# Decode attention over two key/value caches: the order of every engine fixed by hand, and all loads on one queue

## The chip, the cores and the metric

The kernel runs on one core of a Trainium2 chip. The metric is device microseconds of one execution. Most executions of a kernel agree within 0.3%. A profile is one such execution; its span is 1.5 to 2 us shorter than the time of that execution.

Engines: PE multiplies matrices, DVE does elementwise work and reductions, ACT does exponentials and copies, SP issues loads. Sixteen DMA engines move the data. "The end of the stream" is the end of the last K or V packet in the trace's list of DMA packets, and "the tail" is the rest of the span after it.

## The reference, cut to what matters

Two independent decode problems, A and B, with one query each; the outputs stand side by side.

```python
q = (x @ wq).reshape(32 heads, 128)
scores = einsum("hd,hkd->hk", q, k) * 128 ** -0.5     # A: 16384 keys, B: the last 4096
p = softmax(scores)
o = einsum("hk,hkd->hd", p, v)
out = o.reshape(1, 4096) @ wo                          # 512 columns
```

K and V of one A head are 4 MB each; four B heads together are as large. The whole input is 352 MB, read once.

## The kernel before

A chunk is 64 keys on each of 128 partitions, half an A head or two B heads. DVE multiplies K by q and adds the halves, PE sums what is left with an identity matrix (`red`), DVE reduces, ACT takes the exponential, and PE does p.v. with 64 matmuls. A scheduler orders the instructions. K, wq and wo are loaded from SP, V and x from ACT.

```python
def _scores(nc, cx, kv, q_of, pieces):
    ...
        nc.vector.tensor_tensor(out=prod[...], in0=kv[...], in1=q..., op=ALU.mult)      # L73
    nc.vector.tensor_tensor(out=half, in0=prod[..., 0:64], in1=prod[..., 64:128], op=ALU.add)  # L80
    ... 8 matmuls with ident into red                                                   # L90
    nc.vector.tensor_reduce(out=sc, in_=red, ...)                                       # L98
    ... exp on ACT into p_sb, row sums into cs

def _pv(nc, cx, acc, p_sb, vt, cs, first, last):
    o_ps, s_ps = acc
    for c in range(n):
        nc.tensor.matmul(o_ps[0:1, :], lhsT=p_sb[:, c:c+1], rhs=vt[:, c, :], ...)       # L117
    nc.tensor.matmul(s_ps[0:1, 0:1], lhsT=cs, rhs=cx.ones_col[:, 0:1], ...)             # L124

# main loop: head by head; after every fourth A head a group of four B heads
    for h in range(stA.H):
        ...
        _head_A(nc, cx, stA, h)              # K on nc.sync, V on nc.scalar
        if h % (2 * G) == 0:
            _load_wo(nc, cx, stA, h)
        if h % G == G - 1:
            if (h // G) % 2 == 0:
                _load_wo(nc, cx, stB, h - G + 1)
            _group_B(nc, cx, stB, h - G + 1)
```

There are two buffers each for K, V and wo, and one for `s_ps`. `...` on a line of its own, or in an index, marks a cut.

The softmax here doesn't subtract the row's maximum and nothing guards it: scores larger than these inputs give would overflow.

## Time and profile before

858.1 us is the median of four runs (857.0 to 859.0).

| | before |
|---|---|
| span | 855.4 us |
| mean load rate | 413 GB/s |
| DVE busy, PE busy | 69%, 66% |
| end of the stream | 841.1 us |
| tail | 14.3 us |

The page's DMA rows give the busy share in tenths and the rate in 40 slices, and then each queue with its packets, MB and share of the 16 engines:

```profile
DMA  9999999999999899999999999999999999999992
GB/s 392 423 424 379 420 432 432 426 426 427 434 422 435 334 431 439 424 429 419 433 421 437 423 425 431 427 429 409 419 429 427 434 421 428 432 427 430 401 398 87
...
q1 hardware_dynamic: 11684, 184.56, 50.7%
q10 hardware_dynamic: 9504, 167.78, 46.3%
```

The load engines are busy nearly all the time, at about 427 GB/s in most slices. Only the dips and the last slice leave anything to win. Here are the windows of three dips (busy time of each engine, then PE's clock, the DMA share and GB/s):

```profile
60.00:70.00 10.00, 7.73 (x74) 6.59 (x75) 8.48 (x7) 0.78 (x4) 0.00 (x0) 0.70 0.74 282
280.00:290.00 10.00, 4.63 (x34) 2.94 (x34) 9.97 (x6) 0.35 (x2) 0.00 (x0) 0.50 0.68 292
290.00:300.00 10.00, 9.94 (x157) 8.96 (x154) 6.53 (x2) 0.36 (x1) 0.00 (x0) 0.94 0.91 362
```

The end of the chain of waits (start, duration, what) shows the last B heads, one per 2.35 us, and then the output product:

```profile
846.03 0.37 ACT orow L139
846.44 0.29 PE oc_ps L144 x4
846.73 1.32 PE o_ps L117 x22
848.04 0.06 PE s_ps L124 x2
848.19 0.17 DVE recip L137
848.38 0.37 ACT orow L139
...
851.69 1.04 PE outB L156 x4
```

### The profile page before, as it was taken

To read this page: it belongs to the slowest core of one execution; us is meant where nothing else is said; L and a number is where in the kernel's file an instruction comes from. 1 tells how busy PE (TensorE), PEld (TensorE's weight loads), DVE (VectorE), ACT (ScalarE), POOL (GpSimd) and SP (SyncE) were. 2 spreads that over 40 slices of the span, in tenths; PEclk is the share of its full clock that TensorE was granted. 3 is DMA by queue.
4 is the path that set the end of the run, shared out by engine and by line. 5 is a ranking of instruction groups with operands and counts; after the bars stand their busy time and mean duration, and the time that the engine had idled before them with its cause. 6 is when DMAs were issued, how large, how long until landed. Compare 5 with 4: busy or idle time off the path is not lost.

```text
span 855.4 us, 13729 instructions
## 1 busy us (share of the span) xinstructions
PE 565.1 (66%) x6335; PEld 425.1 (50%) x6336; DVE 590.3 (69%) x346; ACT 64.7 (8%) x275; POOL 0.7 (0%) x6
## 2 busy tenths in 40 slices
PE   3146657768782677758755586758877657673877
PEld 1034535565640566446644464536755536453656
DVE  0469775975783866947967397656969378785791
ACT  2000020100010000100000000000001000010001
POOL 0000000000000000000000000000000000000000
PEclk9577888889896699969978897788998779886999
DMA  9999999999999899999999999999999999999992
GB/s 392 423 424 379 420 432 432 426 426 427 434 422 435 334 431 439 424 429 419 433 421 437 423 425 431 427 429 409 419 429 427 434 421 428 432 427 430 401 398 87
DMA packets 21245, 353.20 MB, mean 413 GB/s; under 512 B 2498, under 2 KB 2500, under 8 KB 4548
## 3 DMA queue, kind: packets, MB, share of 16 engines
q1 hardware_dynamic: 11684, 184.56, 50.7%
q10 hardware_dynamic: 9504, 167.78, 46.3%
q8 instruction: 49, 0.80, 0.4%
q14 instruction: 8, 0.07, 0.0%
HBM read 352.32 MB, written 0.00 MB: 412 GB/s over the span
## 4 chain that ended last, share of the span: by engine, by line
DMA 55%; DVE 21%; PE 15%; issue 7%; another core or an unknown queue 1%; ACT 1%; ACTq 0%; SPq 0%; DVEq 0%
DMA kt<-in_A_k_cache_dram 26%; DMA vt<-in_A_v_cache_dram 16%; DVE prod L73 12%; PE o_ps L117 10%; DVE half L80 6%; DMA kt<-in_B_k_cache_dram 6%; DMA xTB<-in_B_x_dram 4%; PE red L90 3%; DMA vt<-in_B_v_cache_dram 3%; DVE sc L98 3%; ACT orow L139 0%; PE oc_ps L144 0%; DVE recip L137 0%; PE outB L156 0%
## 5 line engine op out<-in xcount | busy, mean ns | idle before, releaser
L117 PE MATMUL o_ps<-vt,p_sb 128*1 128x128 bf16 x5120 | 351.9, 236 | 112.2 <-DMA vt<-in_A_v_cache_dram 82.6
L117 PEld LDWEIGHTS <-p_sb 128*1 128x1 bf16 x5120 | 333.9, 92 | 132.8 <-issue 112.1
L73 DVE TENSOR_TENSOR prod<-kt,qallA 128x8192 bf16<-128x8192 bf16 x64 | 282.9, 4420 | 90.4 <-DMA kt<-in_A_k_cache_dram 89.5
L90 PE MATMUL red<-half,ident 128*128 128x512 bf16 x640 | 169.0, 403 | 84.5 <-DVE half L80 84.4
L80 DVE TENSOR_TENSOR half<-prod 128x4096 bf16<-128x4096 bf16 x80 | 182.6, 2283 | 0.6
L90 PEld LDWEIGHTS <-ident 128*128 128x128 bf16 x640 | 58.8, 101 | 124.5 <-issue 69.7
L73 DVE TENSOR_TENSOR prod<-kt,qallB 128x4096 bf16<-128x4096 bf16 x32 | 72.0, 2284 | 11.1 <-DMA kt<-in_B_k_cache_dram 9.4
L98 DVE TENSOR_REDUCE sc<-red 128x64 f32<-128x512 f32 x80 | 54.1, 680 | 37.0 <-PE red L90 35.6
L144 PEld LDWEIGHTS <-orow 1*32 1x32 bf16 x256 | 12.2, 111 | 103.6 <-ACT orow L139 60.1
L139 ACT ACTIVATE orow<-o_ps,recip 1x128 bf16<-1x128 f32 x64 | 22.8, 356 | 514.5 <-DVE recip L137 467.7
L144 PE MATMUL oc_ps<-one,orow 1*32 1x1 bf16 x256 | 17.4, 171 | 54.1 <-ACT orow L139 53.7
L137 DVE RECIPROCAL recip<-s_ps 1x1 f32<-1x1 f32 x64 | 9.6, 150 | 50.1 <-PE s_ps L124 50.1
L102 ACT ACTIVATE p_sb<-sc 128x64 bf16<-128x64 f32 (+1 forms) x96 | 23.4, 244 | 251.8 <-DVE sc L98 251.5
L124 PE MATMUL s_ps<-ones_col,cs 128*1 128x1 f32 x192 | 18.3, 165 | 18.2 <-DVE recip L137 17.6
L153 DVE CAST oc<-oc_ps 128x4 bf16<-128x4 f32 x16 | 2.5, 155 | 39.0 <-PE oc_ps L144 39.0
L124 PEld LDWEIGHTS s_ps<-ones_col,cs 128*1 128x1 f32 x192 | 11.4, 84 | 31.5 <-DVE recip L137 19.7
L45 PE MATMUL q_ps<-wq_t,xbA 128*128 128x512 bf16 x32 | 9.4, 466 | 13.5 <-DVE xbA L40 13.5
L102 ACT ACTIVATION_READ_ACCUMULATOR p_sb<-sc 128x1 f32 x96 | 17.9, 186 | 0.1
L156 PE MATMUL outA<-wo_t,oc 128*1 128x512 bf16 x32 | 12.3, 528 | 4.9 <-DVE oc L153 4.9
L40 DVE COPY xbB<-xTB 128x128 bf16<-128x128 bf16 x4 | 0.6, 222 | 20.1 <-DMA xTB<-in_B_x_dram 20.1
L45 PEld LDWEIGHTS <-xbA 128*128 128x128 bf16 x32 | 3.7, 116 | 18.6 <-DVE xbA L40 13.6
L156 PEld LDWEIGHTS <-oc 128*1 128x1 bf16 x64 | 5.7, 99 | 12.9 <-DVE oc L153 5.8
(17 smaller groups left out, 32.3 us busy)
## 6 DMA issues: line engine op xcount, KB each, us to landing
vt<-in_A_v_cache_dram ACTq DMA_DIRECT2D x32, 4096.0 KB, 22.1
kt<-in_A_k_cache_dram SPq DMA_DIRECT2D x32, 4096.0 KB, 24.2
kt<-in_B_k_cache_dram SPq DMA_DIRECT2D x32, 1024.0 KB, 20.0
vt<-in_B_v_cache_dram ACTq DMA_DIRECT2D x32, 1024.0 KB, 25.0
wq_t<-in_A_wq_dram SPq DMA_DIRECT2D x1, 4096.0 KB, 12.2
wo_t<-in_A_wo_dram SPq DMA_DIRECT2D x4, 1024.0 KB, 21.2
wo_t<-in_B_wo_dram SPq DMA_DIRECT2D x4, 1024.0 KB, 27.5
wq_t<-in_B_wq_dram SPq DMA_DIRECT2D x1, 4096.0 KB, 16.1
```

What stands on the lines that cost most here:

```text
L45: nc.tensor.matmul(q_ps[:, :], lhsT=xb[:, c, :], rhs=wq_t[:, c, j * 512 : (j + 1) * 512], start=(c == 0), stop=(c == KC - 1),)
L73: nc.vector.tensor_tensor(out=prod[:, k0 : k0 + n, :], in0=kv[:, k0 : k0 + n, :], in1=q.rearrange("p (o d) -> p o d", o=1).broadcast_to([P ...
L80: nc.vector.tensor_tensor(out=half[:, :, :], in0=prod[:, :, 0 : DH // 2], in1=prod[:, :, DH // 2 : DH], op=ALU.add,)
L90: nc.tensor.matmul(red[:, :, :], lhsT=cx.ident[:, :], rhs=half[:, :, b * W : (b + 1) * W], start=(b == 0), stop=(b == nb - 1),)
L98: nc.vector.tensor_reduce(out=sc[:, :], in_=red[:, :, :], axis=AX.X, op=ALU.add)
L102: nc.scalar.activation(out=p_sb[:, k0 : k0 + n], in_=sc[:, k0 : k0 + n], func=ACT.Exp, scale=SCALE, accum_out=cs[:, i : i + 1],)
L117: nc.tensor.matmul(o_ps[0:1, :], lhsT=p_sb[:, c : c + 1], rhs=vt[:, c, :], start=(first and c == 0), stop=(last and c == n - 1),)
L124: nc.tensor.matmul(s_ps[0:1, 0:1], lhsT=cs, rhs=cx.ones_col[:, 0:1], start=first, stop=last,)
L137: nc.vector.reciprocal(recip[:, :], s_ps[0:1, 0:1])
L139: nc.scalar.activation(out=orow[:, :], in_=o_ps[0:1, :], func=ACT.Copy, scale=recip[0:1, 0:1])
L144: nc.tensor.matmul(st.oc_ps[32 * hp : 32 * hp + 32, j : j + 1], lhsT=orow_j[:, j, :], rhs=cx.one[0:1, 0:1], start=True, stop=True,)
L156: nc.tensor.matmul(st.out_ps[0:1, :], lhsT=oc[:, j : j + 1], rhs=st.wo_t[:, g, j * st.DN : (j + 1) * st.DN], start=(h == G - 1 and j == 0) ...
```

## The change

Its intent: keep PE from waiting on the softmax of the chunk it has just reduced (p.v. runs one chunk behind), keep the ends of heads out of the way of the loads' releases, and issue every load from SP in the order in which the data is used. `cx.o` pins an instruction to its place in the program. The core of the diff, with cuts:

```diff
+class _Loads:                       # one list of all loads, issued strictly in order
+    def release(self, pool):
+        self.free[pool] += 1
+        self.pump()
+    def pump(self):
+        while self.todo and self.free[self.todo[0][0]]:
+            pool, fn = self.todo.pop(0)
+            self.free[pool] -= 1
+            fn()
...
+    for i, u in enumerate(units):    # a unit: one A head, or a group of four B heads
+        if i < n - 1:
+            ld.add("kt", lambda u=u: _load_kv(nc, cx, u, "k"))
+        if i == n - 2:
+            ld.add("kt", lambda: _load_kv(nc, cx, units[n - 1], "k"))
+        ld.add("vt", lambda u=u, c=(2 if i == n - 1 else 1): _load_kv(nc, cx, u, "v", c))
...
+        if u.st is stA and u.heads[0] % per == 0:          # per = 8
+            ld.add("wo", lambda b=u.heads[0] // per: _load_wo(nc, cx, stA, b))
+        if u.st is stA and u.heads[0] % per == 2:
+            ld.add("wo", lambda b=u.heads[0] // per: _load_wo(nc, cx, stB, b))
...
+    tail_from = len(chunks) - 3
+    for c, ch in enumerate(chunks):
+        _mult(nc, cx, ch)                                  # L144
+        if prev is not None:
+            _softmax(nc, cx, prev)
+            waiting.append(prev)
+        _add(nc, cx, ch)                                   # L156
+        fin_dve()                    # one step of each ended head
+        fin_pe()                     # among them outA/outB, which frees wo (L256)
+        _red(nc, cx, ch)                                   # L169
+        if c <= tail_from:           # p.v. of the last chunks is held back
+            while waiting:
+                fins += pv(waiting.pop(0))                 # L201
+        prev = ch
```

`s_ps` moves into column 128 of `o_ps`, so that a head needs one PSUM bank. The last K is queued before the last two V, and V of the last head is loaded in two halves.

More of the change, by code (lines that the diff above doesn't have):

```diff
@@ L27, with __init__, __call__, add @@
     pass
-def _weights_q(nc, cx, st):
+class _Order:
+    def __init__(self, tc):
+        self.tc = tc
+    def __call__(self, ins):
+        self.tc.keep_in_program_order(ins)
+        return ins
+class _Loads:
+    def __init__(self):
+        self.todo, self.free = [], {}
+    def add(self, pool, fn):
+        self.todo.append((pool, fn))
+    def release(self, pool):
[6 more added lines that the diff above has]
+            fn()
+class _Chunk:
+    def __init__(self, unit, k0, pieces, last_of_unit):
+        self.unit, self.k0, self.pieces, self.last_of_unit = unit, k0, pieces, last_of_unit
+class _Unit:
+    kt = vt = None
+def _load_x(nc, cx, st):
+    D = st.wq.shape[0]
+    KC = D // P
+    xT = cx.singles.tile([P, KC], BF16, tag=f"xT{st.name}", name=f"xT{st.name}")
+    nc.scalar.dma_start(out=xT[:, :], in_=st.x[0, 0, :].rearrange("(p c) -> p c", c=KC))
+    st.xb = cx.singles.tile([P, KC, P], BF16, tag=f"xb{st.name}", name=f"xb{st.name}")
+    for c in range(KC):
+        cx.o(nc.vector.tensor_copy(st.xb[:, c, :], xT[:, c : c + 1].broadcast_to([P, P])))
+def _load_wq(nc, cx, st):
     D, N = st.wq.shape
     KC = D // P
-    xT = cx.singles.tile([P, KC], BF16, tag=f"xT{st.name}", name=f"xT{st.name}")
-    st.dma_x.dma_start(out=xT[:, :], in_=st.x[0, 0, :].rearrange("(p c) -> p c", c=KC))
-    wq_t = cx.vt_pool.tile([P, KC, N], BF16, tag="vt", name="wq_t")
-    nc.sync.dma_start(out=wq_t[:, :, :], in_=st.wq.rearrange("(p c) f -> p c f", c=KC))
-    xb = cx.singles.tile([P, KC, P], BF16, tag=f"xb{st.name}", name=f"xb{st.name}")
-    for c in range(KC):
-        nc.vector.tensor_copy(xb[:, c, :], xT[:, c : c + 1].broadcast_to([P, P]))
+    st.wq_t = cx.kt_pool.tile([P, KC, N], BF16, tag="kt", name="wq_t")
+    cx.o(nc.sync.dma_start(out=st.wq_t[:, :, :], in_=st.wq.rearrange("(p c) f -> p c f", c=KC)))
+def _q(nc, cx, st):
+    D, N = st.wq.shape
+    KC = D // P
     st.qall = cx.singles.tile([P, N], BF16, tag=f"qall{st.name}", name=f"qall{st.name}")
@@ L44, in _weights_q @@
         for c in range(KC):
-            nc.tensor.matmul(
+            cx.o(nc.tensor.matmul(
                 q_ps[:, :],
-                lhsT=xb[:, c, :],
-                rhs=wq_t[:, c, j * 512 : (j + 1) * 512],
+                lhsT=st.xb[:, c, :],
+                rhs=st.wq_t[:, c, j * 512 : (j + 1) * 512],
                 start=(c == 0),
                 stop=(c == KC - 1),
-            )
-        nc.scalar.copy(st.qall[:, j * 512 : (j + 1) * 512], q_ps[:, :])
-def _load_wo(nc, cx, st, h):
-    st.wo_t = cx.wo_pool.tile([P, 2, G * st.DN], BF16, tag="wo", name="wo_t")
-    nc.sync.dma_start(
-        out=st.wo_t[:, :, :],
-        in_=st.wo[h * DH : (h + 2 * G) * DH, :].rearrange(
-            "(g p j) f -> p g (j f)", g=2, j=G
-        ),
-    )
@@ L66, in _scores, with _load_wo @@
-def _scores(nc, cx, kv, q_of, pieces):
-    prod = cx.prod_pool.tile([P, U, DH], BF16, tag="prod", name="prod")
-    for k0, n, q in pieces:
-        nc.vector.tensor_tensor(
-            out=prod[:, k0 : k0 + n, :],
-            in0=kv[:, k0 : k0 + n, :],
+            ))
+        cx.o(nc.scalar.copy(st.qall[:, j * 512 : (j + 1) * 512], q_ps[:, :]))
+    cx.loads.release("kt")
+def _load_wo(nc, cx, st, i):
+    t = cx.wo_pool.tile([P, 2, G * st.DN], BF16, tag="wo", name="wo_t")
+    st.wo_t[i] = t
+    n = 2 * G * DH
+    cx.o(nc.sync.dma_start(
+        out=t[:, :, :],
+        in_=st.wo[i * n : (i + 1) * n, :].rearrange("(g p j) f -> p g (j f)", g=2, j=G),
+    ))
@@ new lines, in _load_kv @@
+def _load_kv(nc, cx, unit, which, cut_last=1):
+    pool, tag = (cx.kt_pool, "kt") if which == "k" else (cx.vt_pool, "vt")
+    t = pool.tile([P, unit.keys, DH], BF16, tag=tag, name=tag)
+    setattr(unit, tag, t)
+    st = unit.st
+    view = st.k_view if which == "k" else st.v_view
+    L = st.W // P
+    n = len(unit.heads)
+    for i, h in enumerate(unit.heads):
+        src = view[h].rearrange("(p l) d -> p l d", p=P)
+        cuts = cut_last if i == n - 1 else 1
+        w = L // cuts
+        for c in range(cuts):
+            cx.o(nc.sync.dma_start(
+                out=t[:, i * L + c * w : i * L + (c + 1) * w, :],
+                in_=src[:, c * w : (c + 1) * w, :],
+            ))
@@ L76, in _scores, with _mult @@
+def _mult(nc, cx, ch):
+    ch.prod = cx.prod_pool.tile([P, U, DH], BF16, tag="prod", name="prod")
+    for k0, n, st, h, _, _ in ch.pieces:
+        q = st.qall[:, h * DH : (h + 1) * DH]
+        cx.o(nc.vector.tensor_tensor(
+            out=ch.prod[:, k0 : k0 + n, :],
+            in0=ch.unit.kt[:, ch.k0 + k0 : ch.k0 + k0 + n, :],
             in1=q.rearrange("p (o d) -> p o d", o=1).broadcast_to([P, n, DH]),
             op=ALU.mult,
-        )
-    half = cx.half_pool.tile([P, U, DH // 2], BF16, tag="half", name="half")
@@ L80, in _scores, with _add, _red @@
-    nc.vector.tensor_tensor(
-        out=half[:, :, :],
-        in0=prod[:, :, 0 : DH // 2],
-        in1=prod[:, :, DH // 2 : DH],
+        ))
+    if ch.last_of_unit:
+        cx.loads.release("kt")
+def _add(nc, cx, ch):
+    ch.half = cx.half_pool.tile([P, U, DH // 2], BF16, tag="half", name="half")
+    cx.o(nc.vector.tensor_tensor(
+        out=ch.half[:, :, :],
+        in0=ch.prod[:, :, 0 : DH // 2],
+        in1=ch.prod[:, :, DH // 2 : DH],
         op=ALU.add,
-    )
+    ))
+def _red(nc, cx, ch):
@@ L86, in _scores @@
     W = 512 // U
     nb = DH // 2 // W
-    red = cx.red_pool.tile([P, U, W], F32, tag="red", name="red")
+    ch.red = cx.red_pool.tile([P, U, W], F32, tag="red", name="red")
     for b in range(nb):
-        nc.tensor.matmul(
-            red[:, :, :],
+        cx.o(nc.tensor.matmul(
+            ch.red[:, :, :],
             lhsT=cx.ident[:, :],
-            rhs=half[:, :, b * W : (b + 1) * W],
+            rhs=ch.half[:, :, b * W : (b + 1) * W],
             start=(b == 0),
             stop=(b == nb - 1),
-        )
+        ))
@@ L97, in _scores, with _softmax @@
+def _softmax(nc, cx, ch):
     sc = cx.small.tile([P, U], F32, tag="sc", name="sc")
-    nc.vector.tensor_reduce(out=sc[:, :], in_=red[:, :, :], axis=AX.X, op=ALU.add)
-    p_sb = cx.small.tile([P, U], BF16, tag="p", name="p_sb")
-    cs = cx.small.tile([P, 2], F32, tag="cs", name="cs")
-    for i, (k0, n, _) in enumerate(pieces):
-        nc.scalar.activation(
-            out=p_sb[:, k0 : k0 + n],
+    cx.o(nc.vector.tensor_reduce(out=sc[:, :], in_=ch.red[:, :, :], axis=AX.X, op=ALU.add))
+    ch.p = cx.small.tile([P, U], BF16, tag="p", name="p_sb")
+    ch.cs = cx.small.tile([P, len(ch.pieces)], F32, tag="cs", name="cs")
+    for i, (k0, n, _, _, _, _) in enumerate(ch.pieces):
+        cx.o(nc.scalar.activation(
+            out=ch.p[:, k0 : k0 + n],
@@ L106, in _scores, with _pv @@
             scale=SCALE,
-            accum_out=cs[:, i : i + 1],
-        )
-    return p_sb, cs
-def _pv(nc, cx, acc, p_sb, vt, cs, first, last):
-    o_ps, s_ps = acc
-    n = p_sb.shape[1]
+            accum_out=ch.cs[:, i : i + 1],
+        ))
+def _pv(nc, cx, ch, i):
+    k0, n, st, h, first, last = ch.pieces[i]
+    if first:
+        st.o_ps[h] = cx.pso_pool.tile([1, DH + 1], F32, tag="o", name="o_ps")
+    o_ps = st.o_ps[h]
     for c in range(n):
-        nc.tensor.matmul(
-            o_ps[0:1, :],
-            lhsT=p_sb[:, c : c + 1],
-            rhs=vt[:, c, :],
+        cx.o(nc.tensor.matmul(
+            o_ps[0:1, 0:DH],
+            lhsT=ch.p[:, k0 + c : k0 + c + 1],
+            rhs=ch.unit.vt[:, ch.k0 + k0 + c, :],
@@ L121, in _pv @@
             start=(first and c == 0),
             stop=(last and c == n - 1),
-        )
-    nc.tensor.matmul(
-        s_ps[0:1, 0:1],
-        lhsT=cs,
-        rhs=cx.ones_col[:, 0:1],
-        start=first,
-        stop=last,
-    )
-def _finish_head(nc, cx, st, h, acc):
-    o_ps, s_ps = acc
+            skip_group_check=True,
+        ))
+        if c == 0:
+            cx.o(nc.tensor.matmul(
+                o_ps[0:1, DH : DH + 1],
+                lhsT=ch.cs[:, i : i + 1],
+                rhs=cx.ones_col[:, 0:1],
+                start=False,
+                stop=last,
+                skip_group_check=True,
+            ))
@@ new lines, in _pv, with _fin_row, _fin_col @@
+    if ch.last_of_unit and i == len(ch.pieces) - 1:
+        cx.loads.release("vt")
+def _fin_row(nc, cx, st, h):
+    o_ps = st.o_ps.pop(h)
+    recip = cx.small.tile([1, 1], F32, tag="recip", name="recip")
+    cx.o(nc.vector.reciprocal(recip[:, :], o_ps[0:1, DH : DH + 1]))
+    orow = cx.small.tile([1, DH], BF16, tag="orow", name="orow")
+    cx.o(nc.scalar.activation(
+        out=orow[:, :], in_=o_ps[0:1, 0:DH], func=ACT.Copy, scale=recip[0:1, 0:1]
+    ))
+    st.orow[h] = orow
+def _fin_col(nc, cx, st, h):
@@ L135, in _finish_head @@
     hp = h % G
-    recip = cx.small.tile([1, 1], F32, tag="recip", name="recip")
-    nc.vector.reciprocal(recip[:, :], s_ps[0:1, 0:1])
-    orow = cx.small.tile([1, DH], BF16, tag="orow", name="orow")
-    nc.scalar.activation(out=orow[:, :], in_=o_ps[0:1, :], func=ACT.Copy, scale=recip[0:1, 0:1])
     if hp == 0:
         st.oc_ps = cx.pst_pool.tile([P, G], F32, tag="ocp", name="oc_ps")
-    orow_j = orow[0:1, :].rearrange("o (a j) -> o j a", j=G)
+    orow_j = st.orow.pop(h)[0:1, :].rearrange("o (a j) -> o j a", j=G)
@@ L143, in _finish_head @@
     for j in range(G):
-        nc.tensor.matmul(
+        cx.o(nc.tensor.matmul(
             st.oc_ps[32 * hp : 32 * hp + 32, j : j + 1],
@@ L149, in _finish_head @@
             stop=True,
-        )
-    if hp == G - 1:
-        oc = cx.small.tile([P, G], BF16, tag="oc", name="oc")
-        nc.vector.tensor_copy(oc[:, :], st.oc_ps[:, :])
-        g = (h // G) % 2
-        for j in range(G):
-            nc.tensor.matmul(
-                st.out_ps[0:1, :],
-                lhsT=oc[:, j : j + 1],
-                rhs=st.wo_t[:, g, j * st.DN : (j + 1) * st.DN],
-                start=(h == G - 1 and j == 0),
-                stop=(h == st.H - 1 and j == G - 1),
-            )
@@ L165, in _acc @@
-def _acc(cx):
-    return (
-        cx.pso_pool.tile([1, DH], F32, tag="o", name="o_ps"),
-        cx.pss_pool.tile([1, 1], F32, tag="s", name="s_ps"),
-    )
-def _head_A(nc, cx, st, h):
-    L = st.W // P
-    kt = cx.kt_pool.tile([P, L, DH], BF16, tag="kt", name="kt")
-    nc.sync.dma_start(out=kt[:, :, :], in_=st.k_view[h].rearrange("(p l) d -> p l d", p=P))
-    vt = cx.vt_pool.tile([P, L, DH], BF16, tag="vt", name="vt")
-    nc.scalar.dma_start(out=vt[:, :, :], in_=st.v_view[h].rearrange("(p l) d -> p l d", p=P))
-    acc = _acc(cx)
-    q = st.qall[:, h * DH : (h + 1) * DH]
-    for u in range(L // U):
-        p_sb, cs = _scores(nc, cx, kt[:, u * U : (u + 1) * U, :], None, [(0, U, q)])
-        _pv(
-            nc, cx, acc, p_sb[:, :], vt[:, u * U : (u + 1) * U, :], cs[:, 0:1],
-            u == 0, u == L // U - 1,
-        )
-    _finish_head(nc, cx, st, h, acc)
@@ L189, in _group_B @@
-def _group_B(nc, cx, st, h0):
-    L = st.W // P
-    kt = cx.kt_pool.tile([P, G * L, DH], BF16, tag="kt", name="kt")
-    vt = cx.vt_pool.tile([P, G * L, DH], BF16, tag="vt", name="vt")
-    for t, view, eng in ((kt, st.k_view, nc.sync), (vt, st.v_view, nc.scalar)):
-        for i in range(G):
-            eng.dma_start(
-                out=t[:, i * L : (i + 1) * L, :],
-                in_=view[h0 + i].rearrange("(p l) d -> p l d", p=P),
-            )
-    per = U // L
-    for u in range(G // per):
-        heads = [h0 + u * per + i for i in range(per)]
-        pieces = [
-            (i * L, L, st.qall[:, h * DH : (h + 1) * DH]) for i, h in enumerate(heads)
-        ]
-        p_sb, cs = _scores(nc, cx, kt[:, u * U : (u + 1) * U, :], None, pieces)
-        for i, h in enumerate(heads):
-            acc = _acc(cx)
-            k0 = u * U + i * L
-            _pv(
-                nc, cx, acc, p_sb[:, i * L : (i + 1) * L], vt[:, k0 : k0 + L, :],
-                cs[:, i : i + 1], True, True,
-            )
-            _finish_head(nc, cx, st, h, acc)
@@ L216, in _store, with _fin_cast, _fin_out @@
-def _store(nc, cx, st, out, at):
-    row = cx.singles.tile([1, st.DN], BF16, tag=f"row{st.name}", name=f"row{st.name}")
-    nc.scalar.copy(row[0:1, :], st.out_ps[0:1, :])
-    nc.sync.dma_start(out=out[0, 0:1, at : at + st.DN], in_=row[0:1, :])
+        ))
+def _fin_cast(nc, cx, st, h):
+    st.oc = cx.small.tile([P, G], BF16, tag="oc", name="oc")
+    cx.o(nc.vector.tensor_copy(st.oc[:, :], st.oc_ps[:, :]))
+def _fin_out(nc, cx, st, h):
+    i, g = h // (2 * G), (h // G) % 2
+    for j in range(G):
+        cx.o(nc.tensor.matmul(
+            st.out_ps[0:1, :],
+            lhsT=st.oc[:, j : j + 1],
+            rhs=st.wo_t[i][:, g, j * st.DN : (j + 1) * st.DN],
+            start=(h == G - 1 and j == 0),
+            stop=(h == st.H - 1 and j == G - 1),
+        ))
+    if g == 1:
+        cx.loads.release("wo")
+    if h == st.H - 1:
+        row = cx.singles.tile([1, st.DN], BF16, tag=f"row{st.name}", name=f"row{st.name}")
+        cx.o(nc.scalar.copy(row[0:1, :], st.out_ps[0:1, :]))
+        cx.o(nc.sync.dma_start(out=cx.out[0, 0:1, st.at : st.at + st.DN], in_=row[0:1, :]))
@@ L243 @@
     cx = _Ctx()
+    cx.o = _Order(tc)
+    cx.out = out
     pool = lambda name, bufs, **kw: ctx.enter_context(tc.tile_pool(name=name, bufs=bufs, **kw))
@@ L253 @@
     cx.red_pool = pool("red", 2, **PS)
-    cx.pso_pool = pool("pso", 2, **PS)
-    cx.pss_pool = pool("pss", 1, **PS)
+    cx.pso_pool = pool("pso", 3, **PS)
     cx.pst_pool = pool("pst", 1, **PS)
     cx.psout_pool = pool("psout", 1, **PS)
+    ld = cx.loads = _Loads()
+    ld.free = {"kt": 2, "vt": 2, "wo": 2}
     cx.one = cx.singles.tile([1, 1], BF16, tag="one", name="one")
-    nc.vector.memset(cx.one[:, :], 1.0)
+    nc.gpsimd.memset(cx.one[:, :], 1.0)
     cx.ones_col = cx.singles.tile([P, 1], F32, tag="ones_col", name="ones_col")
-    nc.vector.memset(cx.ones_col[:, :], 1.0)
+    nc.gpsimd.memset(cx.ones_col[:, :], 1.0)
     ones_mat = cx.singles.tile([P, P], BF16, tag="ones_mat", name="ones_mat")
@@ L274, with problem @@
     )
-    def problem(name, x, k_cache, v_cache, wq, wo, sk0, W):
+    def problem(name, x, k_cache, v_cache, wq, wo, sk0, W, at):
         st = _Problem()
-        st.name, st.x, st.wq, st.wo, st.W = name, x, wq, wo, W
+        st.name, st.x, st.wq, st.wo, st.W, st.at = name, x, wq, wo, W, at
         st.H = k_cache.shape[1]
@@ L283, in problem @@
         st.out_ps = cx.psout_pool.tile([1, st.DN], F32, tag=f"out{name}", name=f"out{name}")
+        st.wo_t, st.o_ps, st.orow = {}, {}, {}
         return st
-    stA = problem("A", A_x, A_k_cache, A_v_cache, A_wq, A_wo, 0, SkA)
-    stB = problem("B", B_x, B_k_cache, B_v_cache, B_wq, B_wo, SkB - WB, WB)
-    stA.dma_x = stB.dma_x = nc.scalar
-    _weights_q(nc, cx, stA)
+    stA = problem("A", A_x, A_k_cache, A_v_cache, A_wq, A_wo, 0, SkA, 0)
+    stB = problem("B", B_x, B_k_cache, B_v_cache, B_wq, B_wo, SkB - WB, WB, A_wo.shape[1])
@@ L291 @@
+    units = []
     for h in range(stA.H):
-        if h == G - 1:
-            _weights_q(nc, cx, stB)
-        _head_A(nc, cx, stA, h)
-        if h % (2 * G) == 0:
-            _load_wo(nc, cx, stA, h)
-        if h % G == G - 1:
-            if (h // G) % 2 == 0:
-                _load_wo(nc, cx, stB, h - G + 1)
-            _group_B(nc, cx, stB, h - G + 1)
-        if h == stA.H - 1:
-            _store(nc, cx, stA, out, 0)
-    _store(nc, cx, stB, out, stA.DN)
+        units.append((stA, [h]))
+        if h % G == G - 1:
+            units.append((stB, list(range(h - G + 1, h + 1))))
@@ new lines @@
+    chunks = []
+    for i, (st, heads) in enumerate(units):
+        u = units[i] = _Unit()
+        u.st, u.heads = st, heads
+        L = st.W // P
+        u.keys = L * len(heads)
+        u.chunks = []
+        for k0 in range(0, u.keys, U):
+            pieces, at = [], 0
+            while at < U:
+                h, off = heads[(k0 + at) // L], (k0 + at) % L
+                n = min(U - at, L - off)
+                pieces.append((at, n, st, h, off == 0, off + n == L))
+                at += n
+            u.chunks.append(_Chunk(u, k0, pieces, k0 + U == u.keys))
+        chunks += u.chunks
@@ new lines @@
+    ld.add("kt", lambda: _load_wq(nc, cx, stA))
+    n = len(units)
+    for i, u in enumerate(units):
[4 more added lines that the diff above has]
+        ld.add("vt", lambda u=u, c=(2 if i == n - 1 else 1): _load_kv(nc, cx, u, "v", c))
+        if i == G - 2:
+            ld.add("kt", lambda: _load_wq(nc, cx, stB))
+        per = 2 * G
+        if u.st is stA and u.heads[0] % per == 0:
+            ld.add("wo", lambda b=u.heads[0] // per: _load_wo(nc, cx, stA, b))
+        if u.st is stA and u.heads[0] % per == 2:
+            ld.add("wo", lambda b=u.heads[0] // per: _load_wo(nc, cx, stB, b))
@@ new lines, with fin_pe, fin_dve @@
+    _load_x(nc, cx, stA)
+    _load_x(nc, cx, stB)
+    ld.pump()
+    _q(nc, cx, stA)
+    fins = []
+    def fin_pe():
+        for f in list(fins):
+            s, st, h = f
+            if s == 1:
+                _fin_col(nc, cx, st, h)
+                f[0] = 2 if h % G == G - 1 else 9
+            elif s == 3:
+                _fin_out(nc, cx, st, h)
+                f[0] = 9
+        fins[:] = [f for f in fins if f[0] != 9]
+    def fin_dve():
+        for f in fins:
+            s, st, h = f
+            if s == 0:
+                _fin_row(nc, cx, st, h)
+                f[0] = 1
+            elif s == 2:
+                _fin_cast(nc, cx, st, h)
+                f[0] = 3
@@ new lines, in pv @@
+    def pv(ch):
+        for i, (_, _, st, h, _, last) in enumerate(ch.pieces):
+            _pv(nc, cx, ch, i)
+            if last:
+                yield [0, st, h]
+    prev = None
+    waiting = []
+    tail_from = len(chunks) - 3
+    for c, ch in enumerate(chunks):
+        if c == 2 * (G - 1):
+            _q(nc, cx, stB)
+        _mult(nc, cx, ch)
[10 more added lines that the diff above has]
+        prev = ch
@@ L307 @@
+    _softmax(nc, cx, prev)
+    waiting.append(prev)
+    for ch in waiting:
+        for i, (_, _, st, h, _, last) in enumerate(ch.pieces):
+            _pv(nc, cx, ch, i)
+            fin_dve()
+            fin_pe()
+            if last:
+                fins.append([0, st, h])
+    while fins:
+        fin_dve()
+        fin_pe()
 _INS = ['A_x', 'A_k_cache', 'A_v_cache', 'A_wq', 'A_wo', 'B_x', 'B_k_cache', 'B_v_cache', 'B_wq', 'B_wo']
```

## The prediction

> **What bounds the kernel now.** The DMA engines. The page's DMA line is at 9 tenths in nearly every slice, mean 413 GB/s; the queues fill 97.4% of the span (50.7%, 46.3%, instruction fetch 0.4%). A 32 KB packet takes 1.22 us and an 8 KB one 0.316 us on each of 16 engines: 427 and 415 GB/s. All packets make about 829 us of 16 engines. The Trainium skill, "HBM Reference", Specifications, gives about 425 GB/s for a core streaming alone; this trace agrees. PE (66%, clock 0.84) and DVE (69%) have slack: per 19.6 us of K and V loading DVE needs 15, PE 11 at full clock. The chain of waits is 55% DMA. The bytes (352 MB) don't change, so only this can be won:
>
> 1. Start: first packet at 1.9 us. Unchanged.
> 2. Gaps. The windows show 282 GB/s at 60-70 us, 292 and 362 at 280-300, 381 and 398 at 590-610, 380 and 338 at 820-840. By packets they cost about 8 us: tiles were released late, or SP was held behind another load.
> 3. Tail. The last load ends near 839 us, the span at 855.4: 16.4 us. The timeline shows p.v of four B heads at one per 2.35 us, serialized by the single s_ps buffer through RECIPROCAL, then 5.0 us from the last p.v to the end.
>
> **What the change does.** The same products, adds and matmuls are moved; DVE and PE busy time stay within 2%. s_ps moves into o_ps's bank, which unties PE from RECIPROCAL. All loads go on SP in order of use. That alone gives no bandwidth: the Trainium skill, "DMA: Bandwidth & Descriptors", "Issuing engines are not separate DMA queues", says loads share 16 engines whoever issues them; here stretches with one queue alone also run at 424-429 GB/s.
>
> Does the one queue run dry? With K landed at T, its second product ends at T+12: K is free early. V is tight: p.v of its second chunk runs after the next head's first add, T+19.6+4.4+0.7+2.3=T+27, then reduction 1.9 and p.v 3.7 at full clock: free at T+32.6; at half clock (3.6 and 5.9) T+36.5. The V two heads on must be issued by about T+37 (four tiles of 9.8 us; issue to first packet 1.0). Margin 4 us at full clock, almost none at half: few, small gaps, 0-4 us in place of 8.
>
> Tail: the last K precedes two V tiles, so all scores are done, and the last head's V lands in halves. After the last packet: landing 1, 16 p.v matmuls 1-1.5, then the same 5.0: 7-8 us, not 16.4. This gain of 8-9 us is all critical.
>
> The earlier first product (24 us, from 34.5) is worth nothing by itself.
>
> Sum (an estimate from trace durations): 1.9 + 829 + 3 + 7.5 = 841 us of span, against 855.4; plus the 2-3 us by which times exceed the span, **843 us**, range **838 to 850**: 1.8% faster, close to the 2% line. Faster 0.41, same 0.57, slower 0.02.
>
> **What would show it.** Last load packet at 831-836 us; tail 7-8.5 us; ten-microsecond windows at 415-435 GB/s, none below 350; DVE's waits still on K loads; one queue at 97-98%.
>
> **What would make it wrong.** PE at half clock for long, so each V is released late and the queue runs dry by a microsecond per head (up to +15 us); bubbles between loads on one queue that the second had hidden; or one queue streaming better than two (up to 4 us less).

## The result

The changed kernel takes 871.2 us (median of four, 869.1 to 873.7), against 858.1. The ratio is 1.0154, with a 95% interval of 1.0124 to 1.0185: slower, though by less than the 2% at which a difference counts as one here. Ratios here are the mean time of one kernel's runs over that of the other's in the same rounds, so they are not quite the ratio of the medians quoted. Executions over 1.5% slower than the fastest of the same kernel are left out of the means.

| | before | changed | predicted |
|---|---|---|---|
| span | 855.4 | 867.4 | 841 |
| first packet | 1.8 | 1.8 | 1.9 |
| end of the stream | 841.1 | 845.5 | 833.9 (1.9 + 829 + 3) |
| tail | 14.3 | 21.9 | 7.5 |
| DVE busy, PE busy (us) | 590.3, 565.1 | 588.4, 567.8 | within 2% |

So 4.4 of the 12.0 us came before the end of the stream, and 7.6 after it. Against the prediction the span is 26.0 us too long: 11.6 before the end of the stream and 14.4 after it. The page's DMA rows after the change:

```profile
DMA  9999999999989999999989999999998999999980
GB/s 387 435 428 417 428 436 426 417 424 417 437 360 434 427 413 439 418 425 422 433 371 433 408 426 426 428 414 430 401 440 362 422 426 418 439 411 416 431 359 2
...
q1 hardware_dynamic: 21044, 352.33, 95.9%
```

The old dips are gone (the windows from 60, 280 and 290 us now hold 437, 420 and 456 GB/s), and new ones stand at regular distances, about 205 us or eight A heads apart. The windows of them:

```profile
240.00:250.00 10.00, 6.36 (x43) 2.78 (x44) 9.06 (x9) 1.43 (x8) 0.00 (x0) 0.58 0.72 288
440.00:450.00 10.00, 1.12 (x3) 0.34 (x4) 8.48 (x7) 1.14 (x6) 0.00 (x0) 0.65 0.87 374
450.00:460.00 10.00, 9.51 (x101) 5.94 (x100) 6.38 (x5) 1.06 (x4) 0.00 (x0) 0.84 0.89 365
650.00:660.00 10.00, 4.16 (x18) 1.31 (x19) 10.00 (x7) 1.14 (x6) 0.00 (x0) 0.50 0.66 262
```

Measured against 427 GB/s, these three places lack 3.3, 2.7 and 3.9 us. In the timeline around the first one (start, duration, engine, line; in brackets the idle time before it and what ended that), SP issues wo just after outA has run, and the next K right behind it:

```profile
236.29 4.42 DVE L144 TENSOR_TENSOR prod<-kt,qallA 128x8192 bf16<-128x8192 bf16 x1 [10.23 <-DMA kt<-in_A_k_cache_dram]
...
243.44 0.15 DVE L250 CAST oc<-oc_ps 128x4 bf16<-128x4 f32 x1
...
243.64 1.86 PE L256 MATMUL outA<-wo_t,oc 128*1 128x512 bf16 x4 [9.67 <-DVE oc L250]
...
245.54 0.38 SPq L115 DMA_DIRECT2D wo_t<-in_A_wo_dram  x1
...
246.01 0.42 SPq L134 DMA_DIRECT2D kt<-in_A_k_cache_dram  x1
```

The view of waits on SP puts a number on SP's own waiting (total, times, longest). The stream lost less than that, since loads issued before kept the DMA engines busy for a while:

```profile
SPq L115 <- PE outA L256: 62.3, 3, 20.8
```

And this is the end of the chain of waits. The last scores are still being made when the stream has ended at 845.5 us, and p.v. of the last three chunks follows in a row on PE:

```profile
844.20 2.21 DVE half L156
846.41 0.04 issue
846.45 3.18 PE red L169 x8
849.63 0.15 PE o_ps L201
849.81 3.60 PE o_ps L201 x64
853.43 1.75 PE o_ps L201 x31
...
860.72 1.77 PE o_ps L201 x31
```

### The profile page after: what moved, and what is told of

Same layout as the page of the kernel before. It is cut to its first block, busy times and chain, and to the rows that moved or that the text cites. A ratio compares the mean times of both kernels' runs of the same rounds, so it can differ in the third digit from the quotient of the medians.

```text
span 867.4 us, 13704 instructions
## 1 busy us (share of the span) xinstructions
PE 567.8 (65%) x6336; PEld 390.7 (45%) x6336; DVE 588.4 (68%) x344; ACT 64.8 (7%) x275; POOL 0.8 (0%) x8
## 4 chain that ended last, share of the span: by engine, by line
DMA 56%; DVE 18%; PE 17%; issue 7%; SPq 1%; ACT 0%; DVEq 0%; ACTq 0%
DMA kt<-in_A_k_cache_dram 53%; PE o_ps L201 9%; DVE prod L144 9%; DVE half L156 7%; PE red L169 6%; DMA xTB<-in_B_x_dram 3%; DVE sc L181 2%; PE outB L256 2%; SPq L134 1%; PE outA L256 1%; SPq L115 0%; DVE oc L250 0%; PE oc_ps L239 0%; DVE recip L225 0%; PE o_ps L210 0%
## 5 line engine op out<-in xcount | busy, mean ns | idle before, releaser
L201 PEld LDWEIGHTS <-p_sb 128*1 128x1 bf16 x5120 | 296.7, 85 | 42.8 <-issue 42.7
L201 PE MATMUL o_ps<-vt,p_sb 128*1 128x128 bf16 x5120 | 314.1, 222 | 1.7 <-DMA vt<-in_A_v_cache_dram 1.7
L169 PE MATMUL red<-half,ident 128*128 128x512 bf16 x640 | 203.2, 475 | 126.7 <-DVE half L156 126.7
L169 PEld LDWEIGHTS <-ident 128*128 128x128 bf16 x640 | 68.4, 114 | 225.5 <-issue 178.9
L181 DVE TENSOR_REDUCE sc<-red 128x64 f32<-128x512 f32 x80 | 54.8, 685 | 12.8 <-PE red L169 12.6
L256 PE MATMUL outA<-wo_t,oc 128*1 128x512 bf16 x32 | 14.1, 591 | 69.3 <-DVE recip L225 59.6
L256 PE MATMUL outB<-wo_t,oc 128*1 128x512 bf16 x32 | 14.1, 590 | 45.6 <-DVE oc L250 45.6
L239 PEld LDWEIGHTS <-orow 1*32 1x32 bf16 x256 | 11.5, 110 | 49.7 <-ACT orow L227 42.1
L225 DVE RECIPROCAL recip<-o_ps 1x1 f32<-1x1 f32 x64 | 9.1, 150 | 28.4 <-PE o_ps L201 28.1
L210 PE MATMUL o_ps<-ones_col,cs 128*1 128x1 f32 x192 | 19.0, 168 | 0.0
L210 PEld LDWEIGHTS o_ps<-ones_col,cs 128*1 128x1 f32 x192 | 14.1, 87 | 1.7 <-issue 1.7
L99 PE MATMUL q_ps<-wq_t,xbB 128*128 128x512 bf16 x32 | 8.2, 378 | 4.7 <-ACT qallB L106 4.7
(17 smaller groups left out, 19.6 us busy)
## 6 DMA issues: line engine op xcount, KB each, us to landing
kt<-in_B_k_cache_dram SPq DMA_DIRECT2D x32, 1024.0 KB, 19.8
wo_t<-in_B_wo_dram SPq DMA_DIRECT2D x4, 1024.0 KB, 16.9
```

Source lines behind the costliest of these rows:

```text
L99: cx.o(nc.tensor.matmul(q_ps[:, :], lhsT=st.xb[:, c, :], rhs=st.wq_t[:, c, j * 512 : (j + 1) * 512], start=(c == 0), stop=(c == KC - 1),))
L169: cx.o(nc.tensor.matmul(ch.red[:, :, :], lhsT=cx.ident[:, :], rhs=ch.half[:, :, b * W : (b + 1) * W], start=(b == 0), stop=(b == nb - 1),))
L181: cx.o(nc.vector.tensor_reduce(out=sc[:, :], in_=ch.red[:, :, :], axis=AX.X, op=ALU.add))
L201: cx.o(nc.tensor.matmul(o_ps[0:1, 0:DH], lhsT=ch.p[:, k0 + c : k0 + c + 1], rhs=ch.unit.vt[:, ch.k0 + k0 + c, :], start=(first and c == 0) ...
L210: cx.o(nc.tensor.matmul(o_ps[0:1, DH : DH + 1], lhsT=ch.cs[:, i : i + 1], rhs=cx.ones_col[:, 0:1], start=False, stop=last, skip_group_chec ...
L225: cx.o(nc.vector.reciprocal(recip[:, :], o_ps[0:1, DH : DH + 1]))
```

## The experiments

Theories at the start. R: the stream's new loss is the wo load, whose buffer comes free too late, and K and V stand behind it in the one queue. Its rival B: bubbles of the single queue, or wo's own small rows. For the tail, D: p.v. is held back. Its rival L: the scores are late since the last A head's K comes late.

| run | time | ratio to before | span | end of stream | tail |
|---|---|---|---|---|---|
| changed | 871.2 | 1.0154 | 867.4 | 845.5 | 21.9 |
| wo later | 866.2 | 1.0077 | 864.7 | 841.9 | 22.8 |
| no holding back | 865.5 | 1.0073 | 863.0 | 847.2 | 15.8 |
| K earlier | 871.8 | 1.0143 | 871.0 | 848.7 | 22.3 |
| these three | 860.6 | 1.0012 | 858.8 | 840.8 | 18.0 |
| wo from ACT | 862.8 | 1.0072 | 863.8 | 840.8 | 23.0 |
| these three, V from ACT | 870.4 | 1.0157 | 867.9 | 848.1 | 19.8 |
| wo later, p.v. first | 857.3 | 1.0001 | 855.4 | 832.6 | 22.8 |
| p.v. first alone | 874.3 | 1.0192 | 870.7 | 849.1 | 21.6 |
| p.v. first, new tail | 847.3 | 0.9887 | 845.7 | 832.9 | 12.8 |
| the same, K not earlier | 851.2 | 0.9930 | 849.4 | 833.3 | 16.1 |
| the same, one head sooner | 846.4 | 0.9869 | 844.1 | 832.6 | 11.5 |

All gave correct results. The time is a median, while the span, the stream and the tail are those of the one profiled run; for the changed kernel this was the fastest of its four (869.1 us). The runs of the table came on three chips, where the kernel before took 859.1 us (wo later, no holding back, K earlier, these three), 856.2 us (wo from ACT, V from ACT, wo later with p.v. first, p.v. first with the new tail) and 857.5 us (the other three). So across calls the ratios are to be compared, and a difference of 2 or 3 us between the times of two calls shows nothing.

### wo queued one head later

```diff
-        if u.st is stA and u.heads[0] % per == 0:
+        if u.st is stA and u.heads[0] % per == 1:
```

> One edit of the changed kernel: each load of A's wo is queued one head later, so that outA of the block before has released the buffer long before. Theory R (release): the three stretches near 245, 450 and 657 us with 102-120 GB/s come from the one in-order queue standing still until outA has run; K and V behind it wait too. Then the three dips vanish, idle time of the DMA engines falls by 8-9 us, and the time falls from 871 to 861-864 us; the tail stays at 22 us. Rival B (bubbles or slow small rows): the dips belong to the wo load itself or to one queue alone; then they move with it and the time stays at 869-872.

Measured: 866.2 us, more than the 861 to 864 expected. The three stops were 9.8 us in sum, but the stream ended only 3.6 us earlier in the two traces; by the ratios the gain is about 6.6 us (an estimate: 0.0077 of 858.1). R is right that the stops go (the window at 240 us is back at 423 GB/s, from 288), but its sum left out what remains. Dips now stand after the groups of B heads:

```profile
350.00:360.00 10.00, 9.51 (x98) 5.94 (x97) 5.45 (x6) 1.06 (x4) 0.00 (x0) 0.84 0.91 369
560.00:570.00 10.00, 7.58 (x110) 6.04 (x107) 6.25 (x6) 1.06 (x4) 0.00 (x0) 1.00 0.90 359
760.00:770.00 10.00, 9.51 (x101) 5.94 (x100) 5.92 (x5) 1.07 (x4) 0.00 (x0) 0.86 0.88 356
```

The timeline before the first of these dips shows what SP's V load waits for:

```profile
340.22 4.42 DVE L144 TENSOR_TENSOR prod<-kt,qallA 128x8192 bf16<-128x8192 bf16 x1 [9.94 <-DMA kt<-in_A_k_cache_dram]
...
347.57 1.86 PE L256 MATMUL outA<-wo_t,oc 128*1 128x512 bf16 x4 [10.96 <-DVE recip L225]
...
349.60 3.59 PE L169 MATMUL red<-half,ident 128*128 128x512 bf16 x8
...
355.11 1.89 PE L201 MATMUL o_ps<-vt,p_sb 128*1 128x128 bf16 x31
...
357.03 0.33 SPq L134 DMA_DIRECT2D vt<-in_A_v_cache_dram  x1
```

From the start of the product to the V load are 16.8 us. PE had been idle for 11 us; outA then took 1.86 us (1.03 at full clock) and the reduction 3.59 (1.90 at full clock), and only then came the p.v. that frees V. The Trainium skill, "TensorE: Matmul & The Clock Gate", "Part 1: The HAM clock gate", says that PE falls to half clock after an idle window of about 3.4 us and needs at least one busy window of that length to come back. The trace agrees: these durations are about doubled, and the granted clock was 0.50 in the stretch from 347.6 to 353.2 us and 1.00 after it, so full clock came back some 5.7 us after outA began. In the changed kernel it came back 4.2 us after outA began, the same group took 16.1 us from the product to the V load, and the window from 350 us on stayed at 428 GB/s. That is one pair of groups: it shows that V goes out at the edge of being late, not where the edge lies. Whether V's late release is the cause is tested below, by putting p.v. first.

### wo issued from ACT

```diff
-    cx.o(nc.sync.dma_start(
+    cx.o(nc.scalar.dma_start(
         out=t[:, :, :],
         in_=st.wo[i * n : (i + 1) * n, :]...
```

> The changed kernel with the eight wo loads issued from ACT, at the same place in the program; K and V stay on the one SP queue. If the three dips at 245, 450 and 657 us are head-of-line blocking (K and V stuck behind a wo load whose buffer isn't free yet), they go although wo is loaded no earlier: 864-867 us, like the run with wo queued later (866.2). If the dips belong to wo's own bytes or small rows, they stay: 870-872. Tail unchanged near 22 us in both.

Measured: 862.8 us, ratio 1.0072, like wo queued later (1.0077); the stream ended at 840.8. (The time is below the 864 to 867 expected, but the kernel before was 2.9 us faster in this call.) In the page's row of GB/s the three low slices of the changed kernel (360, 371 and 362) are back at 431, 435 and 429:

```profile
GB/s 389 437 415 433 424 426 429 398 434 398 433 431 420 425 410 437 394 428 429 417 435 422 429 420 429 435 404 415 407 434 429 427 429 394 443 414 417 434 327 2
```

wo is loaded at the same place with the same rows and bytes, but K and V do not stand behind it. So what cost was standing in line, and rival B falls for these stops. The Trainium skill, "DMA: Bandwidth & Descriptors", "Anatomy of one DMA — SWDGE (gpsimd) path", says that DMA engines do not wait on semaphores and that the wait is on the issuing sequencer. The section is on loads issued from another engine, but SP's 62.3 us of waiting for outA, with K issued 0.5 us after wo, shows just that.

### p.v. no longer held back at the end

```diff
-    tail_from = len(chunks) - 3
+    tail_from = len(chunks)
```

> One edit of the changed kernel: p.v. of the last three chunks is no longer held back until all scores are done. Theory D (deferral): from the last load packet to the end takes 22 us since three chunks of p.v., 11 us of PE, start only after the last reduction. Without it p.v. of A's last chunk and of B's first pair runs earlier: tail 16-18 us, time 865-867. Theory L (late scores): DVE needs four chunks, about 30 us, after the last A head's K lands, which is 30 us before the last packet; what sets the tail is that the last scores are done only 3-4 us after the last packet. If L alone mattered this run would stay at 870-872.

Measured: 865.5 us, as expected, with a tail of 15.8 in place of 21.9. D holds for 6 us. The stream was unchanged or slightly worse (847.2), since wo was not touched.

### The last A head's K one V earlier

```diff
-        if i < n - 1:
+        if i < n - 2:
             ld.add("kt", lambda u=u: _load_kv(nc, cx, u, "k"))
+        if i == n - 3:
+            ld.add("kt", lambda: _load_kv(nc, cx, units[n - 2], "k"))
```

> One edit of the changed kernel: the last A head's K is loaded one V earlier, about 10 us; p.v. is still held back to the end. Theory L: scores are done some 2-3 us before the last packet in place of 3-4 after; with the 11 us of held-back p.v. still behind them the tail is 14-17 us, time 864-867. Theory D alone: tail unchanged near 22 us, 870-872.

Measured: 871.8 us, tail 22.3; nothing gained. That is what D alone had foretold, and L as stated falls. But D is not the sole answer either, for the timeline shows a third cause:

```profile
835.10 2.28 DVE L156 TENSOR_TENSOR half<-prod 128x4096 bf16<-128x4096 bf16 x1
...
839.25 0.27 PE L201 MATMUL o_ps<-vt,p_sb 128*1 128x128 bf16 x1 [6.56 <-DMA vt<-in_A_v_cache_dram]
...
839.40 5.49 PE L201 MATMUL o_ps<-vt,p_sb 128*1 128x128 bf16 x63
...
844.83 1.90 PE L169 MATMUL red<-half,ident 128*128 128x512 bf16 x8
846.83 0.69 DVE L181 TENSOR_REDUCE sc<-red 128x64 f32<-128x512 f32 x1 [4.93 <-PE red L169]
```

The holding back starts one chunk too late. p.v. of the last A head's first chunk stands on PE ahead of a reduction, and PE idles for 6.6 us until its V has landed. The input of the reduction (`half`) was ready at 837.4 us, 7.4 us before the reduction ran at 844.8. DVE then waits 4.9 us for that reduction. It is the same fault as on SP: an engine that runs in order, with something at its head that is not ready.

### These three together

The diff is the sum of wo later, no holding back and K earlier.

> All three edits together. If R, D and L hold and add up, only start, stream and a short tail are left: last packet near 834-837 us, tail 7-9 us, time 844-849, below both kernels. If the pieces overlap or the stream finds another late release, 850-860.

Measured: 860.6 us, ratio 1.0012: level with the kernel before. That is 12 us above the first expectation and just above the second, which had allowed for another late release (850 to 860). The expected sum was too good, for the two reasons just found. V is released late after B's groups (the stream ended at 840.8), and p.v. blocks reductions at the end (tail 18.0, worse than the 15.8 without the earlier K).

### V loads from ACT

```diff
-            cx.o(nc.sync.dma_start(
+            cx.o((nc.sync if which == "k" else nc.scalar).dma_start(
                 out=t[:, i * L + c * w : i * L + (c + 1) * w, :],
```

> The run with all three edits (860.6 us), with the V loads moved to ACT's queue, so that K and V share the engines packet by packet again and neither waits behind the other's release. If one queue as such costs bandwidth (bubbles between loads), the stream is faster: packets of 32 KB back at 1.22 us, time under 856. If only late releases cost, the rate while both queues are full is the same 425-429 GB/s and the time is 857-864.

Measured: 870.4 us, ratio 1.0157, beside 1.0012 with one queue; outside both expectations. The time went in one place: the windows from 100 to 120 us hold 210 and 7 GB/s. The view of waits on ACT for 95 to 125 us shows why:

```profile
ACT qallB L106 <- PE q_ps L99: 25.9, 7, 23.6
```

ACT stood at B's q for 23.6 us, with the V loads behind it in its own order. (PE in turn had stopped in the middle of q, waiting 22.3 us for DVE to read the scores of a chunk, and DVE for the next K.) While both queues were full the rate was 426 GB/s, and the 32 KB packets took 1.221 us in the mean, against 1.222 in the run with p.v. first and one queue, 1.224 before and 1.226 in the changed kernel: two queues give no more bandwidth. Whether two queues would do as well with releases in good order is left open. A version with p.v. first and V from ACT ended in a deadlock.

### p.v. ahead of the reduction, with and without wo later

```diff
+        ended = []
+        if c < len(chunks) - 5 and waiting:
+            ended += pv(waiting.pop(0))
         _add(nc, cx, ch)
         fin_dve()
         fin_pe()
         _red(nc, cx, ch)
+        fins += ended
```

> The run with wo queued later (866.2 us), and p.v. of the chunk before goes ahead of the reduction on PE (but for the last four chunks, whose order is kept). After a group of B, V was released about 16.5 us after the next K landed: outA at half clock 1.9, reduction 3.4-3.6 and p.v. 3.9 stood in a row. With p.v. first it should be released some 5 us sooner, so the small dips after each group (near 150, 355, 455, 560, 660, 765 us) go: last packet 836-838 us in place of 841.9, time 860-863 with the tail still near 22 us. If the dips have another cause, or PE's order now holds DVE back, 865 or more.

> The changed kernel with p.v. ahead of the reduction as the only edit (wo at its old place). outA of the block before now stands behind p.v. on PE, so wo's buffer comes free 2-4 us later and the three dips near 245, 450 and 657 us grow, while the small dips after B's groups go. Theory of one in-order queue: the releases are not additive, the latest one in line counts; 866-871 us, although with wo later the same edit gave 8.9 us. If the two gains simply add, 862.

Measured with wo later: 857.3 us, and the stream ends at 832.6, both better than expected (860 to 863, and 836 to 838). The tail stayed at 22.8. By the ratios the gain over wo later alone is about 6.5 us (an estimate: 0.0076 of 858.1). The same group as above:

```profile
339.91 4.42 DVE L144 TENSOR_TENSOR prod<-kt,qallA 128x8192 bf16<-128x8192 bf16 x1 [9.74 <-DMA kt<-in_A_k_cache_dram]
...
351.29 1.03 PE L256 MATMUL outA<-wo_t,oc 128*1 128x512 bf16 x4
351.49 0.33 SPq L134 DMA_DIRECT2D vt<-in_A_v_cache_dram  x1
```

V goes out 11.6 us after the product starts, in place of 16.8, and the window from 350 us on holds 434 GB/s. So V's late release was the cause of these dips. Without wo later, the same edit gains nothing and rather loses: 874.3 us, ratio 1.0192, beside 1.0154 (the intervals overlap a little), and above the 866 to 871 expected. The trace shows why. outA now runs behind p.v., so that wo goes out 11.7 us after the product starts, in place of 9.3, and the first stop falls from 288 to

```profile
240.00:250.00 10.00, 8.27 (x88) 6.35 (x88) 7.93 (x8) 1.14 (x6) 0.00 (x0) 0.77 0.33 123
```

So the same edit took the ratio from 1.0077 to 1.0001 with wo later in place, and from 1.0154 to 1.0192 without it. On one in-order queue the releases are not a sum; the latest counts.

### A tail ordered by arrival

wo later, p.v. first and K earlier as above, the last A head's V in halves, and PE's last steps such that no reduction stands behind a p.v. that waits:

```diff
-        ld.add("vt", lambda u=u, c=(2 if i == n - 1 else 1): _load_kv(nc, cx, u, "v", c))
+        ld.add("vt", lambda u=u, c=(2 if i >= n - 2 else 1): _load_kv(nc, cx, u, "v", c))
...
+        left = len(chunks) - 1 - c
+        if left > 4 or left < 2:          # p.v. before the reduction
+            if waiting:
+                ended += pv(waiting.pop(0))
         _add(nc, cx, ch)
         ...
         _red(nc, cx, ch)
+        if left in (3, 4):                # after it
+            ended += pv(waiting.pop(0))
```

> wo later, p.v. first, the last A head's K loaded one V earlier, its V in halves, and PE's last steps ordered by the arrival of data: no reduction stands behind a p.v. that waits for its V. Last packet 835-838 us; tail 9-12 us (scores done about when the last packet lands, then p.v. of one B pair, then the 5 us of the end); time 847-853: faster than both kernels, by 0.7-1.3% than the one before. If the tail is bound by DVE's last chunks instead, 855-860.

> The best run so far (847.3 us, tail 12.8) without the earlier load of the last A head's K: wo later, p.v. first, V in halves and PE's last steps in order of arrival are kept. With K 10 us later, DVE's last four chunks end 8-10 us later: tail 18-21 us, time 853-856. If PE's order alone had made the gain, 847-849.

> The best run so far with one more edit: p.v. of the first B head of the last pair but one goes ahead of the last reduction, into some 1.5 us in which PE stood idle. The tail shrinks by 1.5-2.5 us to 10.5-11.5, time 844.8-846.5. If DVE's last add or V's arrival bounds it, no change: 847.

Measured: 847.3 us (ratio 0.9887), at the lower end of what was expected. In part this was luck: the stream ended earlier than expected (832.9, not 835 to 838) and the tail was longer (12.8, not 9 to 12). Without the earlier K the tail is 16.1 (851.2 us, ratio 0.9930), 3.3 us longer. So once PE's order is right the earlier K is worth something, though less than the 5 to 8 us expected; the intervals of the two ratios overlap a little, so this rests on the tails of two traces. The other two edits of the tail, PE's order and V in halves, were not tested one without the other. With one B head's p.v. ahead of the last reduction the tail is 11.5 and the time 846.4 (ratio 0.9869, interval 0.9848 to 0.9890), both as expected. Its four runs (845.8 to 846.8) lie below those of the version without (847.0 to 847.6), but the interval holds the other's ratio: the last 1 us is not shown. By its median it is the best version, 1.3% faster than the kernel before and, by the two ratios, 2.8% faster than the changed one. What is left of its tail, from the chain of waits:

```profile
831.46 1.75 PE o_ps L201 x31
...
834.11 1.75 PE o_ps L201 x31
835.86 0.86 PE outA L256 x4
...
837.12 1.77 PE o_ps L201 x31
```

PE is the last: p.v. of three B heads and A's output product.

## Why the prediction was wrong

The prediction was 843 us, range 838 to 850, and the measured time is 871.2. Point by point:

1. **The bound, the bytes and the rate: right.** DVE's waits are on K loads as forecast. The one queue moved 32 KB packets in 1.226 us (1.224 before). With the late releases mended, the stream ended at 832.6 to 833.3 us, where the prediction had put it (831 to 836).
2. **"DVE and PE busy time stay within 2%", "the earlier first product is worth nothing": right.** 590.3 to 588.4 and 565.1 to 567.8 us; the first product started at 23.7 us, from 34.5, and the time rose; what the earlier start is worth was not tested alone.
3. **"Few, small gaps, 0-4 us in place of 8": wrong.** This step asked K and V when they come free, and left wo out. In one queue, wo's wait is everybody's: 9.8 us in three stops, where the prediction allowed 0 to 4 us for all gaps together. The run with wo from ACT shows that it was the standing in line.
4. **"V is tight ... margin 4 us at full clock, almost none at half": right in kind, too generous in size.** By the prediction's sum, V was free 16.9 us after the next K at half clock (36.5 - 19.6) and needed by 17.4. In the traces a V load 16.8 us after the product's start dipped and one after 16.1 us did not, and outA (1.0 to 1.9 us) had been left out of the line in front of it. In the changed kernel this loss was small beside wo's; it came to light when the stops of wo were gone, and p.v. first removed it (about 6.5 us by the ratios).
5. **"The last K precedes two V tiles, so all scores are done": wrong.** This step and the next make the largest error, 14.4 us of tail (21.9 against 7.5). DVE needs about 7.4 us for each of four chunks after the last A head's K lands at 816.4 us, 29 us before the stream ends. That sum was never made. The last reduction ended at 849.6 us, 4 us after the stream.
6. **The held-back p.v. was not costed.** "After the last packet: 16 p.v. matmuls" took p.v. as done by then; the code puts three chunks of it after the last reduction, about 11 us of PE, with the output product of A and the ends of heads between them. The sum of the trace is 4.1 us to the end of the last reduction, 12.9 to the end of the last p.v. and 4.9 to the end of the span: 17.0 us where the prediction had 2 to 2.5. Without holding back the tail fell by 6.1 us.
7. **"Then the same 5.0 us": right.** 4.9 us from the last p.v. (862.5) to the end.
8. **"serialized by the single s_ps buffer": true, but worth little.** Untied, a B head still takes 2.14 us (858.41 to 860.55 in the chain), of which p.v. is 1.9; it was 2.35. PE itself sets the pace.

The named ways to fail had half clock in them, but neither the order within the load queue nor that within PE.

## What to carry to other kernels

When loads or matmuls are pinned into one in-order queue, make a table of every entry, small ones too: when is it needed, and when does what it waits for end, at the slow clock. One late wo of 1 MB stopped 8 MB per head behind it, and a p.v. waiting for its V stopped a reduction that DVE was waiting for. Mend the latest release in line first: here p.v. first gained 0.0076 in the ratio once wo was mended, and nothing before. For a kernel bound by its stream, add up every engine's work between the last input's arrival and the end of the stream before saying that only the last piece remains.

## What the Trainium skill lacked or had wrong

- "DMA: Bandwidth & Descriptors", "Issuing engines are not separate DMA queues", says that issuing from several engines only saves issue time. On bandwidth the runs agree (426 GB/s with both queues full; 32 KB packets 1.22 us with one or two). What it lacks: a second queue also keeps a load with a late buffer from holding up the others. The eight wo loads moved to ACT, at the same place in the program, took the ratio from 1.0154 to 1.0072.
- The same page does not warn of the reverse: loads on an engine that also computes stand behind its work. With V on ACT, one wait of 23.6 us stopped the stream (210 and 7 GB/s in two windows).
- The same page, "Queues, rings and completion order", says that an engine drains a packet of typically 9 to 17 descriptors from one ring before it switches. In the trace of the kernel before, the 128 pieces of x, 8 bytes each, start in eight rounds of 16, one round every 1.22 us, and in each of these rounds 16 pieces of wq, 32 KB each, start too. So the two queues seem to alternate piece by piece on each engine (the trace does not name the engine), and the 1 KB x took 12.3 us to land.
- "TensorE: Matmul & The Clock Gate" agrees with the runs (a reduction of eight 512-column matmuls takes 3.59 us after an idle stretch, 1.90 in full clock). No page says what that does to a load queue: buffers are released later just after PE has been idle, and in the one pair of groups compared here 16.8 us was a dip and 16.1 was not.
